# Pooling the keys and values of two batches on TensorE, alpha's load on another queue, and new numbers in the schedule's table

## The chip, the cores and the metric

One core of a Trainium2 chip runs the whole program. The metric is the device time of one execution in microseconds (us), the median of several runs. Engines are named as the profile names them: PE (TensorE), DVE (VectorE), ACT (ScalarE), POOL (GpSimd) and SP, which issues most of the transfers.

## The reference

Attention over pooled keys and values (8 batches, 8 heads, 576 tokens, 64 wide, groups of 8 tokens averaged to 72), then a dense layer pair with a leaky ReLU whose slope alpha is one number per hidden unit, then a layer of 8 experts in which each token goes to one.

```python
k_p = k.reshape(B, H, Sp, pool, D).mean(axis=3)          # 576 -> 72
v_p = v.reshape(B, H, Sp, pool, D).mean(axis=3)
attn = softmax(np.matmul(q, k_p.T) / sqrt(D))
x = np.matmul(attn, v_p)                                  # 4608 x 512
h = x @ w_in                                              # 512 x 2048
x = (max(h, 0) + alpha * min(h, 0)) @ w_out               # 2048 x 512
expert_idx = argmax(x @ w_gate);  gate_w = softmax at expert_idx
out = gate_w * (max(x @ w1[e], 0) @ w2[e])                # 512 x 1024 x 512, e = expert_idx
```

## The kernel before

Every operand of a large product is split into a high and a low float16 part, and each product is three matmuls (high by high, high by low, low by high). The 4608 tokens are 36 tiles of 128; two tiles make a block of 256, of which there are 18. A block's way is: queries scaled and split (tile `qs`), transposed by a DMA (`qT`), scores against the pooled keys (`sc`), eight exponentials on ACT, weights split (`Abuf`), transposed by a DMA (`AT`), the product with the values (`xp`), its split (`xT`), then 16 groups of 12 matmuls into `hp` (line 811), the leaky ReLU on ACT and DVE (`r`, line 829), its split `gT`, and 8 groups of 12 matmuls into `yp` (line 856). The result is split (`x`), transposed (`x2T`), gated (`gp`, `rp`), and its rows are stored to DRAM (`x2d`) with a table of who goes where. After the last block the expert stage gathers 128 rows at a time (`srec`, `x2g`, `x2gT`) and runs lines 1286 and 1304.

Before a block can run, things must be prepared by DVE, POOL and ACT:

- The keys and values of a batch: `plan_batch` loads `raw` (two large halves each for batch 0, eight pieces of one head each for the others), sums 8 rows to one into `kp` (DVE line 439, or POOL lines 443 and 445, whichever the planner picks), takes the largest value over all partitions (`over_all`: DVE `dg`, PE `mp`, line 313), and splits `kp` into `kc` (transposed into `KTb`) and `VSb`, `vlo`.
- `w_in` and `w_out`: `plan_w` rounds the float32 weights in pieces of 128x1024 (`w_in_t`, `w_out_t`: ACT lines 715, 719, 724, DVE lines 727, 731 and 183), finds scales through `over_all`, and splits them (`w_in_hl`, `w_out_hl`).
- The expert weights, spread over the whole first part (`ew`, `eo`, `wsc`).
- alpha and `w_gate`: `alpha_ld`, lines 387 and 389, two loads on SP's queue.

The order of the work on each engine is fixed when the kernel is built. `Plan.emit` is a list scheduler: each piece of work has an engine or a choice of engines, an assumed duration, a key and buffers to acquire and release, and the planner repeatedly takes the piece that can start first by its own clock. Its clock for SP uses the two dictionaries at the top of the file: `ISSUE`, how long SP is held by one issue of a kind, and `LATE`, how much later than the modelled transfer a kind lands. An engine then runs its list strictly in that order, so what the numbers change is the order alone. PSUM holds two buffers with the tag `y`, used by `yp`, and SBUF two with the tag `raw`.

Of the kernel before, what the change touches and what calls it, by code (L numbers as in the profile page):

```python
# [27 lines left out]

ISSUE = {"qT": 1.4, "AT": 1.9, "yT": 1.4, "kT": 1.5, "xT": 1.4, "v": 1.6, "tok": 0.8}
LATE = {"kv": 1.5, "q": 1.0, "ew": 2.5, "st": 1.0, "qT": 1.0, "AT": 1.2, "yT": 1.0, "kT": 0.8, "v": 2.0, "x2": 2.0, "xT": 1.0}  # L30

# [105 lines left out]
def attn_moe_moe_kernel(ctx: ExitStack, tc: tile.TileContext, q, k, v, w_in, w_out, alpha,  # L137
# [217 lines left out]

    o_c1 = add("POOL", 3.6, setup_consts, key=-1000)
    o_c2 = add("POOL", 2.0, setup_consts2, key=0)
# [28 lines left out]
    def alpha_ld():  # L386
        Y.dma_start(out=al1, in_=alpha.rearrange("(m p) -> p m", p=128))
        sm_["g"] = wk.tile([128, KD, NE], F32, tag="wgf", name="g", bufs=1)
        Y.dma_start(out=sm_["g"], in_=w_gate.rearrange("(k p) e -> p k e", p=128))

# [17 lines left out]

    o_al = add("SP", 1.12, alpha_ld, key=-52)
    o_al = add("DVE", tiny(3), alpha_a, [o_al], key=-10)  # L410
# [9 lines left out]
    def plan_batch(b, dl, users):  # L420

        kp, st, raws = [None, None], {}, {}
        red = []
        nc_, pl = (2, "big") if b == 0 else (8, "raw")
        hn = H // nc_
        for w in range(2):
            for c in range(nc_):
# [18 lines left out]
                o = add("SP", dmat(72 * 2048 * hn), load, kind="kv", key=dl - 28 + (8 * w + c) * 8 / nc_, acq=[(pl, 1)])
                red.append(add(EITHER, (0.15 + hn * 0.87, pool(448 * hn) + 0.6), reduce, [o] + red[-1:],
                               key=dl - 26 + (8 * w + c) * 8 / nc_, rel=[(pl, 1)], acq=[("kp", 1)] if c == 0 else []))
# [33 lines left out]
        def vdma():  # L482
            Y.dma_start(out=VS[b][SP_:128, 0], in_=VS[b][0:128 - SP_, 0])
            Y.dma_start(out=VS[b][0:2 * SP_ - 128, 1], in_=VS[b][128 - SP_:SP_, 0])

        osc = {}
        for ws in (((0,), (1,)) if b == 0 else ((0, 1),)):
# [4 lines left out]
            for w in ws:  # L492
                osc[w] = o
        oSK[b], oSV[b] = osc[0], osc[1]
        o = osc[0]
        o1 = add(ANY, his(512), lambda e: s_hi(kc[0:SP_, :, 0, :], kp[0], s_[0], e), [o], key=dl - 7, acq=[("kc", 1)])
        o2 = add(EITHER, stt(512), lambda e: s_lo(kc[0:SP_, :, 1, :], kc[0:SP_, :, 0, :], kp[0], s_[0], e), [o1], key=dl - 6,
                 rel=[("kp", 1)])
        o3 = add("DVE", 0.22, lambda: V.tensor_copy(kc[0:SP_, :, 3, :], kc[0:SP_, :, 0, :]), [o1], key=dl - 6)
        o4 = add("DVE", 0.22, lambda: V.tensor_copy(kc[0:SP_, :, 2, :], kc[0:SP_, :, 1, :]), [o2], key=dl - 5)  # L500
        oKT[b] = add("SP", 1.2, kT, [o2, o3, o4], kind="kT", key=dl - 4 - SPQ, acq=[("KT", 1)], rel=[("kc", 1)])
        o = osc[1]
        o1 = add(ANY, his(512), vhi, [o], key=dl - 4, acq=[("VS", 1)])
        o2 = add(EITHER, stt(512), vlo, [o1], key=dl - 4, acq=[("vlo", 1)], rel=[("kp", 1)])
        o3 = add("SP", 0.5, vdma, [o1], kind="v", key=dl - 4)
        o4 = add("SP", 0.3, lambda: Y.dma_start(out=VS[b][2 * SP_ - 128:3 * SP_ - 128, 1], in_=st["vlo"]), [o2],
                 key=dl - 3, rel=[("vlo", 1)])
# [156 lines left out]
    def plan_w(src, name, col, dl0, dl1, after):  # L664
# [39 lines left out]
        for c in range(8):  # L704
# [72 lines left out]
        for c in range(8):  # L777
# [679 lines left out]
```

## Time and profile before

| | us |
|---|---|
| median of 3 runs (1385.79 to 1389.69) | 1389.04 |
| the profiled execution's own time | 1391.88 |
| its span, first to last instruction | 1390.1 |
| PE busy in the span | 1248.7 (90%) |
| DVE busy | 889.8 (64%) |
| POOL busy | 731.8 (53%) |
| ACT busy | 569.1 (41%) |

The profile is one execution. A busy time counts an engine as busy from an instruction's start to its end; matmuls overlap, so the row of a run of matmuls (its length divided by its count) tells the pace better than the mean of one. "Idle before" is the time in which the engine had nothing running, with the event that ended it. The granted clock is the share of full speed that PE was allowed.

### The profile page before, as it was taken

To read this page: it belongs to the slowest core of one execution; us is meant where nothing else is said; L and a number is where in the kernel's file an instruction comes from. 1 tells how busy PE (TensorE), PEld (TensorE's weight loads), DVE (VectorE), ACT (ScalarE), POOL (GpSimd) and SP (SyncE) were. 2 spreads that over 40 slices of the span, in tenths; PEclk is the share of its full clock that TensorE was granted. 3 is DMA by queue.
4 is the path that set the end of the run, shared out by engine and by line. 5 is a ranking of instruction groups with operands and counts; after the bars stand their busy time and mean duration, and the time that the engine had idled before them with its cause. 6 is when DMAs were issued, how large, how long until landed. Compare 5 with 4: busy or idle time off the path is not lost. (4 is left out here: it accounts for less than half of the span.)

```text
span 1390.1 us, 30446 instructions
## 1 busy us (share of the span) xinstructions
PE 1248.7 (90%) x11555; PEld 868.0 (62%) x11555; DVE 889.8 (64%) x2039; ACT 569.1 (41%) x1309; POOL 731.8 (53%) x788
## 2 busy tenths in 40 slices
PE   0158899999999998999999999998999999999996
PEld 0147465765676565577657766675676776776774
DVE  6999888977888895898878776752432322322321
ACT  3887455545555364566546645530010110110110
POOL 7899757676678577678655655441212212122111
PEclk9999999999999999999999999998999999999999
DMA  9983595896897778778766746539379533883325
GB/s 242 295 239 73 115 243 130 189 234 136 178 221 177 157 183 168 167 183 236 177 143 160 187 125 158 131 91 307 82 206 267 146 77 76 240 260 82 85 66 191
DMA packets 314502, 237.19 MB, mean 171 GB/s; under 512 B 258351, under 2 KB 267695, under 8 KB 309488
## 3 DMA queue, kind: packets, MB, share of 16 engines
q1 hardware_dynamic: 306800, 214.98, 62.6%
q0 software_dynamic: 7552, 20.23, 4.7%
q8 instruction: 92, 1.51, 0.5%
q14 instruction: 58, 0.48, 0.1%
HBM read 263.52 MB, written 54.34 MB: 229 GB/s over the span
## 5 line engine op out<-in xcount | busy, mean ns | idle before, releaser
L811 PE MATMUL hp<-xT,w_in_hl 128*128 128x256 f16 x3456 | 395.9, 275 | 6.2 <-DVE r L829 3.9
L856 PE MATMUL yp<-w_out_hl,gT 128*128 128x512 f16 x1728 | 388.8, 383 | 1.2 <-DVE x L203 1.2
L811 PEld LDWEIGHTS <-w_in_hl 128*128 128x128 f16 x3456 | 336.6, 99 | 53.3 <-issue 6.8
L856 PEld LDWEIGHTS <-gT 128*128 128x128 f16 x1728 | 167.1, 99 | 201.6 <-issue 12.8
L1286 PE MATMUL hp<-x2gT,ws 128*128 128x128 f16 x3744 | 217.6, 221 | 9.8 <-DMA x2gT<-x2g 7.5
L1286 PEld LDWEIGHTS <-ws 128*128 128x128 f16 x3744 | 215.4, 99 | 14.9 <-DMA ws<-wsc 5.6
L1304 PE MATMUL op<-ws,ht 128*128 128x512 f16 x936 | 206.0, 380 | 0.0
L1292 ACT ACTIVATE hr<-hp 128x512 f32<-128x512 f32 x78 | 46.6, 597 | 368.9 <-PE hp L1286 356.8
L842 POOL TENSOR_TENSOR gT<-r,gT 128x512 f16<-128x512 f32 x101 | 121.5, 1207 | 74.1 <-ACT gT L837 70.9
L1304 PEld LDWEIGHTS <-ht 128*128 128x128 f16 x936 | 90.9, 98 | 105.9 <-issue 1.0
L1261 POOL DMA_INDIRECT x2g<-x2d,srec x41 | 44.8, 1092 | 190.7 <-DMA srec<-table 87.5
L829 DVE SCALAR_TENSOR_TENSOR r<-r,al,hp 128x256 f32<-128x256 f32 x288 | 123.2, 470 | 20.7 <-ACT r L825 20.3
L443 POOL TENSOR_TENSOR raw<-raw 72x256 f32<-72x256 f32 (+3 forms) x150 | 115.7, 772 | 38.8 <-DMA raw<-in_v_dram 17.2
L580 ACT ACTIVATE e<-sc,nb,esc 128x72 f32<-128x72 f32 x288 | 116.3, 418 | 46.5 <-DVE nb L572 19.3
L188 ACT ACTIVATE eo<-ew,es 128x512 f16<-128x512 f32 x125 | 83.6, 715 | 117.4 <-DMA wsc<-eo 44.2
L1314 POOL DMA_INDIRECT out_dram<-so,srec x39 | 40.0, 1026 | 165.3 <-DVE so L1311 60.1
L1296 DVE CAST ht<-hr 128x512 f16<-128x512 f32 x78 | 33.6, 431 | 143.3 <-ACT hr L1292 135.0
L1311 DVE TENSOR_SCALAR so<-op,cb 128x512 f32<-128x512 f32 x39 | 29.3, 751 | 144.3 <-PE op L1304 138.4
L837 ACT ACTIVATE gT<-r 128x512 f16<-128x512 f32 x142 | 89.6, 633 | 65.3 <-DVE r L829 31.7
L825 ACT ACTIVATE r<-hp 128x512 f32<-128x512 f32 x144 | 86.1, 599 | 64.7 <-PE hp L811 33.8
L206 POOL TENSOR_TENSOR eo<-ew,eo 128x512 f16<-128x512 f32 x71 | 87.5, 1232 | 5.9
L205 POOL TENSOR_SCALAR ew<-ew,es 128x512 f32<-128x512 f32 x71 | 53.0, 746 | 60.4 <-ACT eo L188 59.9
(227 smaller groups left out, 1477.4 us busy)
## 6 DMA issues: line engine op xcount, KB each, us to landing
ws<-wsc SPq DMA_DIRECT2D x166, 1024.0 KB
ew<-in_moe_w_dram SPq DMA_DIRECT2D x32, 1024.0 KB
wsc<-eo SPq DMA_DIRECT2D x64, 512.0 KB
x2d<-x SPq DMA_DIRECT2D x36, 256.0 KB
qr<-in_q_dram SPq DMA_DIRECT2D x32, 256.0 KB
w_in_f<-in_moe_w_in_dram SPq DMA_DIRECT2D x16, 512.0 KB
w_out_f<-in_moe_w_out_dram SPq DMA_DIRECT2D x16, 512.0 KB
raw<-in_k_dram SPq DMA_DIRECT2D x56, 144.0 KB
```

Source lines behind the costliest of these rows:

```text
L188: A.activation(out=hi, in_=src, func=ACTF.Copy, scale=s)
L206: G.tensor_tensor(out=lo, in0=src, in1=hi, op=ALU.subtract)
L443: G.tensor_tensor(out=r[:, :, 0:n], in0=r[:, :, 0:n], in1=r[:, :, n:2 * n], op=ALU.add)
L580: A.activation(out=c["e"][x], in_=c["scv"][x], func=ACTF.Exp, bias=c["nb"][:, z // 4, z % 4:z % 4 + 1], scale=c["esc"], accum_out=c["sm"][x])
L811: T.matmul(out=hp, lhsT=wt[:, a, kk, (m % 4) * 128:(m % 4 + 1) * 128], rhs=xTt[j][:, x, kk, :], start=(n == 0), stop=(n == 3 * KD - 1))
L825: A.activation(out=c["r"], in_=hps[j, m // 2], func=ACTF.Relu, scale=-1.0)
L829: V.scalar_tensor_tensor(out=c["r"][:, z], in0=c["r"][:, z], scalar=al1[:, m - 1 + z:m + z], in1=hps[j, m // 2][:, z], op0=ALU.mult, op1=A ...
L837: A.activation(out=gT[j][0][:, n2], in_=c["r"], func=ACTF.Copy)
L842: on(eng).tensor_tensor(out=gT[j][1][:, n2], in0=c["r"], in1=gT[j][0][:, n2], op=ALU.subtract)
L856: T.matmul(out=ypt[i], lhsT=gT[j][x][:, m, o_ * 128:(o_ + 1) * 128], rhs=W["w_out"][part][:, w, m % 4, :], start=(m == 0 and x == 0 and w ...
L1286: T.matmul(out=hp[:, f, :], lhsT=ws[kk // 2][:, kk % 2, a, ff * 128:(ff + 1) * 128], rhs=c["xT"][:, x * KD + kk, :], start=(z == 0), stop= ...
L1304: T.matmul(out=op, lhsT=c["ht"][:, x, f, :], rhs=ws[f // 4][:, f % 4, w, :], start=(f == 0 and x == 0 and w == 0), stop=(f == KF2 - 1 and ...
```

## The change

Four things are changed.

1. The pooling of batches 0 and 1 is done by PE: eight matmuls with a 72x72 float32 identity (`idf`) add the eight rows of a group in PSUM (`pool_pe`). The sum lies in a `y` buffer (`kpp`) until it is split. As it is in PSUM, POOL takes no part in the split: the high parts may go to DVE or ACT, the low parts go to DVE.
2. alpha and `w_gate` are loaded from ACT's queue, first thing.
3. The identity `idf` is made by POOL from `idb`, and stays in one of two `x2T` buffers until batch 1 is pooled.
4. The numbers of the planner's table and a few assumed durations are others. They change no instruction, only the order and, where there is a choice, the engine.

```diff
-ISSUE = {"qT": 1.4, "AT": 1.9, "yT": 1.4, "kT": 1.5, "xT": 1.4, "v": 1.6, "tok": 0.8}
-LATE = {"kv": 1.5, "q": 1.0, "ew": 2.5, "st": 1.0, "qT": 1.0, "AT": 1.2, "yT": 1.0, "kT": 0.8, "v": 2.0, "x2": 2.0, "xT": 1.0}
+ISSUE = {"qT": 1.3, "AT": 3.5, "yT": 1.3, "kT": 1.4, "xT": 1.3, "v": 1.6, "v2": 0.85, "tok": 0.4}
+LATE = {"kv": 1.2, "q": 2.0, "ew": 2.1, "st": 1.0, "qT": 0.5, "AT": 2.2, "yT": 0.5, "kT": 0.2, "v": 3.3, "v2": 1.4, "x2": 0.5, "xT": 1.0}
...
+    NPE = 2
+    PEK = 100.0
...
     def stt(n):
-        return dve(n) + 0.02, 0.2 + n * (PHI + PTT)
+        return dve(n) + 0.15, 0.25 + n * (PHI + PTT)
...
+        idf.append(wk.tile([SP_, SP_], F32, tag="x2T", name="idf", bufs=2))
+        G.tensor_copy(idf[0], idb[0:SP_, 0:SP_])
...
     def alpha_ld():
-        Y.dma_start(out=al1, in_=alpha.rearrange("(m p) -> p m", p=128))
+        A.dma_start(out=al1, in_=alpha.rearrange("(m p) -> p m", p=128))
...
-        Y.dma_start(out=sm_["g"], in_=w_gate.rearrange("(k p) e -> p k e", p=128))
+        A.dma_start(out=sm_["g"], in_=w_gate.rearrange("(k p) e -> p k e", p=128))
...
-    o_al = add("SP", 1.12, alpha_ld, key=-52)
+    o_al = add("ACT", 7.0, alpha_ld, key=-1000, lat=2.0)
...
+        by_pe = b < NPE
...
+                def pool_pe(w=w, c=c):
+                    if c == 0:
+                        kp[w] = ps_y.tile([128, DM], F32, tag="y", name="kpp")[0:SP_].rearrange("p (h d) -> p h d", d=D)
+                    r = raws.pop((w, c))
+                    for i in range(PL):
+                        T.matmul(out=kp[w][:, hn * c:hn * c + hn, :], lhsT=idf[0], rhs=r[:, :, i * D:(i + 1) * D],
+                                 start=(i == 0), stop=(i == PL - 1))
...
+                if by_pe:
+                    red.append(add("PE", pe(8, 4 * hn * D * 1.3), pool_pe, [o, o_c1] + red[-1:], key=dl - 26 + (8 * w + c) * 8 / nc_ - PEK,
+                                   rel=[(pl, 1)] + ([("x2T", 1)] if b == NPE - 1 and w == 1 and c == nc_ - 1 else []),
+                                   acq=[("y", 1)] if c == 0 else [], lat=0.15))
+                    continue
-                red.append(add(EITHER, (0.15 + hn * 0.87, pool(448 * hn) + 0.6), reduce, [o] + red[-1:],
+                red.append(add(EITHER, (0.15 + hn * 0.87, pool(448 * hn) + 0.95), reduce, [o] + red[-1:],
...
+        kpr = [("y" if by_pe else "kp", 1)]
+        en, en2 = (ANY, EITHER) if not by_pe else (("DVE", "ACT"), "DVE")
```

**The start of SP's queue.** Here stand K and V of batch 0 (`raw`), the first two query tiles (`qr`), alpha (`al`), `w_gate` (`g`) and the first weights (`w_in_f`). Before:

```order
L431 DMA raw_113<-in_k_dram 72x4x512
L431 DMA raw_115<-in_k_dram 72x4x512
L534 DMA qr<-in_q_dram 128x8x64 x2
L387 DMA al_88<-in_moe_alpha_dram 128x16x1
L389 DMA g<-in_moe_w_gate_dram 128x4x8
L431 DMA raw_135<-in_v_dram 72x4x512
L431 DMA raw_145<-in_v_dram 72x4x512
L692 DMA w_in_f_170<-in_moe_w_in_dram 128x4x256 x2
```

With the change:

```order
L438 DMA raw_118<-in_k_dram 72x4x512
L438 DMA raw_120<-in_k_dram 72x4x512
L561 DMA qr<-in_q_dram 128x8x64 x2
L438 DMA raw_137<-in_v_dram 72x4x512
L438 DMA raw_154<-in_v_dram 72x4x512
L719 DMA w_in_f_158<-in_moe_w_in_dram 128x4x256 x2
L561 DMA qr<-in_q_dram 128x8x64
```

The two small loads are gone from SP, where they stood ahead of V and of `w_in`; they are ACT's first two rows.

**PE's queue from its start to the first groups of the first block.** `kpp` is a pooled sum (x8 is one group of eight matmuls, 72x256 a half of batch 0, 72x64 one head of batch 1), `mp` a largest value over partitions, `xp` attention times values, `hp` the first layer. With the change:

```order
L458 MATMUL kpp<-raw_118,idf 72x256 x8
L458 MATMUL kpp<-raw_120,idf 72x256 x8
L315 LDWEIGHTS ones
L315 MATMUL mp<-dg,ones 128x256
L458 MATMUL kpp<-raw_137,idf 72x256 x8
...
L647 MATMUL xp<-AT,VSb 64x128
L458 MATMUL kpp<-raw,idf 72x64 x16
L838 LDWEIGHTS w_in_hl
L838 MATMUL hp<-xT,w_in_hl 128x256
...
L458 MATMUL kpp<-raw,idf 72x64 x8
L838 LDWEIGHTS w_in_hl
```

Before, PE's queue begins with `mp` and has no row of this kind. Of the sixteen groups of batch 1, seven stand ahead of the first `hp` and nine among the `hp` rows of the first two blocks, each in PE's fixed order behind the load of its piece.

**SP's queue at the change from the last block to the experts.** `srec` is the table's row list for one gather, `x2T` the last block's transpose for the gate, `x2gT` a gathered tile's transpose, `ws` the expert weights. Before:

```order
L1254 DMA srec<-table 128x2
L889 DMA_TRANSPOSE x2T<-x_12635 128x8x128
L1274 DMA_TRANSPOSE x2gT<-x2g 128x8x128 x2
...
L1248 DMA ws_1_12697<-wsc 128x4096
L892 DMA x2d<-x_12635 128x1024
...
L1254 DMA srec<-table 128x2
L889 DMA_TRANSPOSE x2T<-x_12756 128x8x128
```

With the change:

```order
L1281 DMA srec<-table 128x2
L916 DMA_TRANSPOSE x2T<-x_12702 128x8x128
...
L1281 DMA srec<-table 128x2
L919 DMA x2d<-x_12702 128x1024
L1301 DMA_TRANSPOSE x2gT<-x2g 128x8x128 x2
L916 DMA_TRANSPOSE x2T<-x_12842 128x8x128
...
L1275 DMA ws_1_12862<-wsc 128x4096
```

The later `srec` loads, which stood behind weights and the store of `x2d`, now stand ahead of them (five in a row between the two `x2T`), and the last `x2T` stands ahead of the second walk's weights.

## Rows read from the trace of the kernel before

**Rows 1.** Busy by stage: length, PE PEld DVE ACT POOL, clock, DMA share, GB/s.

```profile
0.00:88.70 88.70, 8.58 (x104) 6.86 (x105) 75.66 (x129) 55.73 (x97) 72.64 (x81) 1.00 1.01 265
88.70:160.00 71.30, 62.95 (x504) 47.42 (x504) 68.74 (x115) 48.23 (x77) 62.59 (x56) 0.94 0.40 99
160.00:620.00 460.00, 431.99 (x3574) 287.72 (x3573) 377.15 (x907) 245.62 (x634) 322.22 (x383) 0.98 0.81 185
620.00:940.00 320.00, 316.35 (x2623) 214.99 (x2622) 235.12 (x595) 171.48 (x422) 187.13 (x189) 1.00 0.61 156
940.00:1000.00 60.00, 50.20 (x511) 37.05 (x510) 20.30 (x71) 6.24 (x11) 12.61 (x12) 0.89 0.73 211
1000.00:1390.00 390.00, 378.62 (x4245) 274.01 (x4243) 112.84 (x227) 41.82 (x71) 74.67 (x70) 0.99 0.55 152
```

**Rows 2.** Timeline of PE, 60 to 90: start, length, work, idle before, releaser.

```profile
79.20 1.12 PE L561 MATMUL sc<-KTb,qT 128*128 128x72 f16 x16 [10.46 <-ACT e L580]
...
85.40 1.06 PE L620 MATMUL xp<-AT,VSb 128*64 128x128 f16 x16 [2.59 <-DVE mr L316]
...
88.77 1.44 PE L811 MATMUL hp<-xT,w_in_hl 128*128 128x256 f16 x6 [1.25 <-DVE xT L203]
```

**Rows 3.** DVE by shape, 0 to 90: count, busy us, mean ns, idle before.

```profile
L439 DVE TENSOR_REDUCE kp<-raw 72x256 f32<-72x2048 f32 x2 | 7.2, 3610 | 6.3 <-DMA raw<-in_k_dram 6.3
...
L309 DVE TENSOR_SCALAR dg<-idb,iw 128x128 bf16<-128x128 bf16 x4 | 4.2, 1051 | 0.0
...
L203 DVE SCALAR_TENSOR_TENSOR xT<-xp,xT 128x512 f16<-128x512 f32 x2 | 1.4, 680 | 0.0
...
L439 DVE TENSOR_REDUCE kp<-raw 72x64 f32<-72x512 f32 x1 | 1.0, 1015 | 0.0
```

**Rows 4.** The page's groups: POOL's pooling.

```profile
L443 POOL TENSOR_TENSOR raw<-raw 72x256 f32<-72x256 f32 (+3 forms) x150 | 115.7, 772 | 38.8 <-DMA raw<-in_v_dram 17.2
```

**Rows 5.** Timeline of SP, 0 to 30.

```profile
3.95 4.95 SPq L387 DMA_DIRECT2D al<-in_moe_alpha_dram  x1
8.94 1.71 SPq L389 DMA_DIRECT2D g<-in_moe_w_gate_dram  x1
...
11.68 2.59 SPq L692 DMA_DIRECT2D w_in_f<-in_moe_w_in_dram  x3
```

**Rows 6.** Timeline of DVE, one row, at 30.87.

```profile
30.87 0.24 DVE L309 TENSOR_SCALAR dg<-idb,kvm 128x128 bf16<-128x128 bf16 x1
```

**Rows 7.** Timeline of PE: one shape early and late, and a run of scores.

```profile
15.41 0.37 PE L313 MATMUL mp<-dg,ones 128*128 128x256 bf16 x1 [15.41 <-DVE inv L281]
...
139.70 0.27 PE L313 MATMUL mp<-dg,ones 128*128 128x256 bf16 x1
...
208.05 0.68 PE L561 MATMUL sc<-KTb,qT 128*128 128x72 f16 x16
```

**Rows 8.** The page's groups: weight loads of PE.

```profile
L811 PEld LDWEIGHTS <-w_in_hl 128*128 128x128 f16 x3456 | 336.6, 99 | 53.3 <-issue 6.8
```

**Rows 9.** Timeline of PE, 140 to 172.

```profile
141.12 10.52 PE L856 MATMUL yp<-w_out_hl,gT 128*128 128x512 f16 x48
...
156.01 1.12 PE L561 MATMUL sc<-KTb,qT 128*64 128x72 f16 x16 [3.74 <-DMA KTb<-kc]
157.07 10.37 PE L856 MATMUL yp<-w_out_hl,gT 128*128 128x512 f16 x36
```

**Rows 10.** Waits of PE, 160 to 620: total us, times, longest us.

```profile
PE xp L620 <- DMA AT<-Abuf: 8.5, 5, 4.4
PE mp L313 <- DVE xT L203: 6.1, 4, 3.6
PE rp L973 <- DVE oh L945: 5.5, 4, 1.8
```

**Rows 11.** What POOL waited for, 930 to 1000.

```profile
POOL x2g L1261 <- DMA srec<-table: 35.6, 4, 16.6
```

More of the change, by code (lines that the diff above doesn't have):

```diff
@@ L331, in key_out @@
         return (32 * (i // 2) + 16 if i > 3 else 32 + 16 * (i // 2)) + 8 * (i % 2)
+    idf = []
     def setup_consts():
@@ L354, in setup_consts2 @@
         G.memset(Sacc, 0.0)
-    o_c1 = add("POOL", 3.6, setup_consts, key=-1000)
+    o_c1 = add("POOL", 3.6, setup_consts, key=-1000, acq=[("x2T", 1)])
     o_c2 = add("POOL", 2.0, setup_consts2, key=0)
@@ L484, in vdma, with st_ @@
             Y.dma_start(out=VS[b][0:2 * SP_ - 128, 1], in_=VS[b][128 - SP_:SP_, 0])
+        kpr = [("y" if by_pe else "kp", 1)]
+        en, en2 = (ANY, EITHER) if not by_pe else (("DVE", "ACT"), "DVE")
+        dhi = his(512) if not by_pe else his(512)[1::-1]
+        dlo = stt(512) if not by_pe else stt(512)[0]
+        def st_(f):
+            return f if not by_pe else lambda: f("DVE")
         osc = {}
@@ L495, in plan_batch @@
         o = osc[0]
-        o1 = add(ANY, his(512), lambda e: s_hi(kc[0:SP_, :, 0, :], kp[0], s_[0], e), [o], key=dl - 7, acq=[("kc", 1)])
-        o2 = add(EITHER, stt(512), lambda e: s_lo(kc[0:SP_, :, 1, :], kc[0:SP_, :, 0, :], kp[0], s_[0], e), [o1], key=dl - 6,
-                 rel=[("kp", 1)])
+        o1 = add(en, dhi, lambda e: s_hi(kc[0:SP_, :, 0, :], kp[0], s_[0], e), [o], key=dl - 7, acq=[("kc", 1)])
+        o2 = add(en2, dlo, st_(lambda e: s_lo(kc[0:SP_, :, 1, :], kc[0:SP_, :, 0, :], kp[0], s_[0], e)), [o1], key=dl - 6,
+                 rel=kpr)
         o3 = add("DVE", 0.22, lambda: V.tensor_copy(kc[0:SP_, :, 3, :], kc[0:SP_, :, 0, :]), [o1], key=dl - 6)
@@ L502, in plan_batch @@
         o = osc[1]
-        o1 = add(ANY, his(512), vhi, [o], key=dl - 4, acq=[("VS", 1)])
-        o2 = add(EITHER, stt(512), vlo, [o1], key=dl - 4, acq=[("vlo", 1)], rel=[("kp", 1)])
+        o1 = add(en, dhi, vhi, [o], key=dl - 4, acq=[("VS", 1)])
+        o2 = add(en2, dlo, st_(vlo), [o1], key=dl - 4, acq=[("vlo", 1)], rel=kpr)
         o3 = add("SP", 0.5, vdma, [o1], kind="v", key=dl - 4)
-        o4 = add("SP", 0.3, lambda: Y.dma_start(out=VS[b][2 * SP_ - 128:3 * SP_ - 128, 1], in_=st["vlo"]), [o2],
+        o4 = add("SP", 0.3, lambda: Y.dma_start(out=VS[b][2 * SP_ - 128:3 * SP_ - 128, 1], in_=st["vlo"]), [o2], kind="v2",
                  key=dl - 3, rel=[("vlo", 1)])
@@ L739, in plan_w @@
             if by_dve:
-                o = add("DVE", dve(1024), f2, [o3], key=key - 2, rel=[("eo", 1)])
+                o = add("DVE", dve(1024) + 0.2, f2, [o3], key=key - 2, rel=[("eo", 1)])
                 o = add("DVE", dve(1024), f2b, [o], key=key - 2, rel=[(tk, 1), ("big", 1)])
@@ L794, in plan_w @@
             o = p1 = add(ANY, his(1024), hi, [o_sc, p1], key=first(key - 1, 122), acq=[("big", 1)] if c % 2 == 0 else [])
-            o = add(EITHER, stt(1024), lo, [o], key=first(key - 1, 91), rel=[("big", 1)] if c % 2 == 1 else [])
+            o = add(EITHER, (1.55, 3.95), lo, [o], key=first(key - 1, 91), rel=[("big", 1)] if c % 2 == 1 else [])
             oW[name] += [o, o]
```

## The prediction

> **What bounds the kernel now.** I read the busy time by stage first, then PE's waits and timeline in each stage, because every stage has another limit [rows 1]. Up to 88.7 us PE is busy for 8.6: it has nothing to multiply until the first two tiles of `xT` exist. In that stretch DVE is busy 75.7 of 88.7 and POOL 72.6, and the DMA engines are full (share 1.01). From 88.7 to 160 PE is busy 62.9 of 71.3, DVE 68.7. From 160 to 620 PE is busy 432.0 of 460 and DVE 377.2. From 620 on PE is all but full, save for the change to the experts (50.2 of 60) and the tail. So PE's idle time is 80.1 + 8.3 + 28.0 + 3.7 + 9.8 + 11.4 = 141 us, and what the change is worth is what it takes out of these, less what it adds to PE where PE is full.
>
> The first product starts at 88.77, released by DVE's write of the second `xT` [rows 2]. The `xp` ahead of it stood at 85.40 behind other rows of PE's queue, and the scores at 79.20 behind ACT's exponentials. DVE is nevertheless the engine to count: it hardly rests, and each of those steps waits for a DVE row somewhere.
>
> **Part A, the start.** The change takes from DVE, ahead of the second `xT`, two sums of 3.61 and one of 1.02 [rows 3], and adds the two residuals `kc` and `vlo`, now from PSUM, for which I take the residual of `xT` from PSUM, 0.68 each [rows 3]: -8.2 + 1.4 = -6.9. Other rows change sides too, by the table of numbers; pricing those that differ by their shape's mean, they give back about 1.9 (two multiplications of `e` and a high part of `w_in` leave; the first rows of `w_out` come forward). Net on DVE: -5. DVE starts later: its first rows used to be ready when K landed at 6.3 [rows 3]; now it begins with the table's rows, which wait for POOL's constants, at about 8 by my estimate: +2. Against that, SP loses 4.95 + 1.71 = 6.7 us of issue ahead of V and `w_in` [rows 5], so that `w_in`, issued at 11.68 before, goes out some 6 us earlier. ACT, where the two loads now stand, had no work in that time, so there they cost nothing; if an exponential or a `qs` stood behind them, they would cost up to those 6.7. The transfers are limited by the engines that carry them, so I count 3 of the 6.7. Sum: -5 + 2 - 3 = **-6** (bounds 0, if the exponentials on ACT set the pace, and -12, if all of SP's 6.7 and DVE's 5 come through).
>
> The four large groups on PE cost nothing as long as PE waits there anyway. They could make K late: at the start PE takes 0.37 for a 128x256 float16 product that takes 0.27 at 139.70 [rows 7], 0.10 more, as 256 columns take at 1.2 and not 2.4 GHz (256/1.2 - 256/2.4 = 107 ns), though the clock column has 1.00 there [rows 1]. DVE needs 3.61 for one half of K [rows 3]; eight matmuls of four times 256 columns at the slow level would be 6.8 us for a half, 4 x 256 / 1.2 each. The second half can't start before POOL's or DVE's did, so K could come some us later; but K's next steps stood behind V's sums on DVE, which are gone, so I count nothing.
>
> On how DVE and POOL hinder each other the rows say this: a `dg` takes 1.05 on the mean of the first 90 us and 0.24 alone [rows 3, 6]. POOL loses all of batch 0 and 1, sixteen pieces of two adds of 0.77 and one more add [rows 4], so DVE may also be held less. I leave it out of the sum; it is a rival below. The Trainium skill (SBUF — State Buffer, who interferes with whom) says that the port pair which DVE and GpSimd share is an exclusive lock, held for a whole instruction, so that the later one blocks fully. By that rule DVE's rows would shrink as POOL's go, and the start would come earlier than my sum has it; the two `dg` rows agree with it.
>
> **Part B, 88.7 to 160.** Nine groups of batch 1 now stand in PE's queue among the first products. No row of the trace is a float32 matmul. The nearest is a run of scores, sixteen matmuls of 72 columns in 0.68, 0.042 each with the weight loads hidden [rows 7]. Lower bound: as that, 8 x 0.042 = 0.34 a group. Upper bound: four times the columns (the factor that the new planner line has) and every weight load of 0.099 [rows 8] in the open, 8 x 4 x (0.042 + 0.099) = 4.5. I take 1.2, near four times the score row (1.36), because in the score row the loads are hidden: 9 x 1.2 = +11. Against it: PE's 8.3 us of waits in this stretch are partly filled by just these groups, and batch 1's keys are ready earlier. Its `KTb` now costs a wait of 3.74, after which 36 products took 10.37, 0.288 each, while 48 ran at 0.219 each just before [rows 9]: 2.5 us more, with the granted clock of the stretch at 0.94 [rows 1]. So 10.8 us are to be had there; I take -9. Sum of B: **+2** (bounds -6 and +32). The added wait is for the load of each piece; behind it in PE's queue stands everything. And the two `y` buffers are held by the sums until DVE's `kc` and `vlo` are written, so the first `yp` waits for those: 132 `hp` matmuls stand between the last group and that `yp`, so I count nothing.
>
> **Part C, 160 to 620.** PE's waits there are 28.0 us [rows 1], above all for `AT` (8.5), for `mp` behind `xT` (6.1) and for `rp` behind the gate's DVE rows (5.5) [rows 10]. The new numbers give a transpose of `AT` 3.5 of SP's time and 2.2 of lateness, so the planner puts more products between the scores and `xp`. Counting PE's matmuls in both orders, that distance grows by about 1 us for most tiles, and the one between `gp` and `rp` by about as much. Waits of 1.5 on the mean are cut, not removed: I take a fifth, **-6** (bounds -14, half of them, and +5, since every list is reordered and new waits may come).
>
> **Part D, the change to the experts.** PE idles 9.8 us there [rows 1]; POOL's gathers wait 35.6 us for `srec`, once 16.6 [rows 11]. The `srec` loads now go out ahead of weights and stores. A gather that is earlier helps PE only if its transpose is too: **-3** (bounds -8 and +4).
>
> Sum: -6 + 2 - 6 - 3 = **-13**, and 1391.9 - 13 = 1379 for the profiled execution. That execution was 2.8 above the median of the runs shown, so against the median: 1389 - 13 = **1376**.
>
> **Rivals.**
> - *The start is paid back.* PE is the limit from 88.7 on, so the 11 us of float32 work come off the gains of A, and the new order brings C and D nothing: -6 + 11 - 5 = 0, **1389**. For it: PE is busy 88% in B; the DMA engines are full, so the earlier `w_in` may land no earlier. Against it: DVE, which holds the waits of B, loses work.
> - *Slower: the weight loads of the float32 matmuls lie open.* A group then costs 4.5 and nine 40: -6 + 40 - 9 - 6 - 3 = +16, **1405**. It decides from about 2.7 us a group, where nine groups eat the 24 us that the other terms give. For it: a group alternates eight small products with eight loads of the same identity, and loads have no cheaper row than 0.099 [rows 8]. Against it: the score row hides a load per 0.042 [rows 7]. The Trainium skill (TensorE: Matmul & The Clock Gate, weight-path perf modes) has a rule against this change: fast weight load is off when the type is float32. By it, loads would be dearer than those of the score row; no row here shows one.
> - *POOL's relief sets DVE free.* If DVE's rows shrink as in [rows 6] against [rows 3], four `dg` alone give 3.2 before the start, and the pieces that are longer beside POOL as much again: A becomes -12, B -4, C -8, D -3: -27, **1362**. For it: batch 1's adds on POOL alone are up to 16 x 2 x 0.77 = 25 us [rows 4]. Against it: POOL takes up other rows at once, since the planner gives it what is free.
>
> **How the numbers follow.** A measurement of this kernel tells about 0.3% (4.2 us) from no change. The forecast has 0.50, the third rival 0.20, the first 0.16, the second 0.14. So faster 0.71, same 0.15, slower 0.14. The range reaches from the third rival with 2 us more, 1360, to the first rival and the upper bounds of C or D, 1396; it leaves out the full second rival, and some of the forecast's tails.
>
> **What would show it.** Right: the first `hp` released at 80 to 85 by the second `xT`; groups of `kpp` of about 1.2 us at 72x64, with waits for their loads under 1 us; the wait for `KTb` at 156 gone; PE's idle time from 160 to 620 at 20 to 24; POOL's waits for `srec` under half. Wrong: a first `hp` at 88 or later; groups over 2.7 us; PE waiting for `raw`, or `yp` for `vlo`; or more idle time on PE after 160 than 28.

## The result, and the profile after

The change is slower: its runs lie at 1.0085 of the runs of before, 95% interval 1.0061 to 1.0109, with a median of 1402.29 us (1400.41 to 1404.54, four runs) against 1387.41. The forecast was 1376, its range ended at 1396. The profiled execution took 1400.41 us with a span of 1398.5, 8.4 more than the span of before. The medians lie further apart, since the profiled execution of before (1391.88) lies above its listed runs; the account that follows sets spans against spans.

The change by stage (columns as in [rows 1]; the first stage ends where the first run of `hp` starts, at 95.79 instead of 88.77):

```profile
0.00:95.70 95.70, 49.34 (x279) 35.30 (x280) 70.43 (x138) 62.24 (x112) 57.75 (x63) 1.00 1.00 261
95.70:160.00 64.30, 63.07 (x633) 53.12 (x632) 58.02 (x101) 42.92 (x61) 48.28 (x35) 1.00 0.37 91
160.00:620.00 460.00, 433.10 (x3565) 289.74 (x3564) 371.72 (x897) 249.33 (x640) 300.70 (x356) 0.99 0.81 182
620.00:940.00 320.00, 310.53 (x2606) 212.66 (x2605) 238.38 (x586) 170.03 (x419) 187.99 (x195) 0.99 0.63 156
940.00:1000.00 60.00, 47.55 (x436) 32.81 (x434) 23.21 (x88) 5.87 (x12) 13.55 (x14) 0.89 0.74 211
1000.00:1390.00 390.00, 389.97 (x4368) 281.89 (x4366) 115.93 (x233) 43.55 (x73) 75.07 (x71) 1.00 0.55 148
```

And `kpp` alone, the pooling on PE, over the first 160 us:

```profile
0.00:50.00 50.00, 27.88 (x64) 15.23 (x64) 2.77 (x4) 1.34 (x2) 1.00 1.02 243
50.00:95.70 45.70, 14.27 (x112) 13.73 (x112) 0.00 (x0) 0.00 (x0) 1.00 0.97 280
95.70:160.00 64.30, 11.05 (x147) 10.59 (x145) 2.85 (x4) 1.25 (x2) 1.00 0.37 91
```

So the pooling takes 53.2 us of PE. PE's idle time up to 160 was 88.5 [rows 1] and is 46.4 + 1.2 = 47.6: 40.9 of the 53.2 lie in it. Behind 160 PE idled 52.9 and idles 57.4 (26.9 + 9.5 + 12.5 + 0.0, and 8.5 in the tail). PE's other work is 8.3 shorter (1240.4 against 1248.7). 53.2 - 40.9 + 4.5 - 8.3 = +8.5, the 8.4 of the spans. (The mean granted clock of the profiled executions was 0.987 with the change and 0.983 before, so the clock isn't what the change lost.)

Most of the idle time that is new lies between 590 and 740; before, and with the change:

```profile
590.00:740.00 150.00, 147.06 (x1275) 102.73 (x1274) 124.88 (x305) 87.25 (x225) 104.36 (x114) 1.00 0.73 182
...
590.00:740.00 150.00, 137.54 (x1128) 92.61 (x1127) 126.01 (x293) 76.74 (x195) 99.99 (x122) 0.98 0.76 170
```

PE idles 12.5 us there instead of 2.9.

PE's timeline of the change at the start:

```profile
6.70 13.90 PE L458 MATMUL kpp<-raw,idf 72*72 72x256 f32 x32 [6.70 <-DMA raw<-in_k_dram]
...
20.61 7.03 PE L458 MATMUL kpp<-raw,idf 72*72 72x256 f32 x16
...
27.54 7.05 PE L458 MATMUL kpp<-raw,idf 72*72 72x256 f32 x16
...
79.23 0.26 PE L315 MATMUL mp<-dg,ones 128*128 128x128 bf16 x1 [6.48 <-DVE xT L203]
79.86 4.10 PE L458 MATMUL kpp<-raw,idf 72*72 72x64 f32 x32 [0.37 <-DMA raw<-in_k_dram]
83.75 1.17 PE L588 MATMUL sc<-KTb,qT 128*128 128x72 f16 x16
89.30 1.07 PE L647 MATMUL xp<-AT,VSb 128*64 128x128 f16 x16 [4.37 <-DMA AT<-Abuf]
91.89 4.11 PE L458 MATMUL kpp<-raw,idf 72*72 72x64 f32 x32 [1.53 <-DMA raw<-in_k_dram]
95.79 6.62 PE L838 MATMUL hp<-xT,w_in_hl 128*128 128x256 f16 x48
102.25 1.20 PE L458 MATMUL kpp<-raw,idf 72*72 72x64 f32 x16
```

Each float32 matmul shows as two records, so x16 is one group of eight. Scores that stood at 79.20, `xp` at 85.40 and `hp` at 88.77 [rows 2] now stand at 83.75, 89.30 and 95.79, with two groups of batch 1 (4.1 us) ahead of the scores and two more, behind a wait for `raw`, ahead of `hp`.

What PE waited for from 160 to 620 (columns as in [rows 10]):

```profile
PE gp L947 <- DMA x2T<-x: 13.8, 6, 4.3
PE xp L647 <- DMA AT<-Abuf: 3.6, 3, 1.8
PE hp L838 <- DVE r L856: 3.0, 3, 1.8
PE rp L1000 <- DVE oh L972: 2.6, 3, 1.1
```

The same from 620 to 1000:

```profile
PE hp L1313 <- DMA x2gT<-x2g: 8.5, 1, 8.5
PE gp L947 <- DMA x2T<-x: 7.7, 2, 4.4
```

The waits of [rows 10] are down (`AT` 8.5 to 3.6, `rp` 5.5 to 2.6, `mp` behind `xT` gone), and one has grown that was small before: `gp`, the gate, waits for its `x2T`. From 160 to 620 before, and in the stretch from 590 to 740 of the change, where it makes up most of the 12.5 us:

```profile
PE gp L920 <- DMA x2T<-x: 3.7, 2, 2.1
...
PE gp L947 <- DMA x2T<-x: 9.2, 3, 4.4
```

### The profile page after: what moved, and what is told of

The parts are those of the page before. It is cut to its first block, busy times and chain, and to the rows that moved or that the text cites. A ratio compares the mean times of both kernels' runs of the same rounds, so it can differ in the third digit from the quotient of the medians.

```text
span 1398.5 us, 31059 instructions
## 1 busy us (share of the span) xinstructions
PE 1293.6 (92%) x11875; PEld 905.5 (65%) x11875; DVE 878.4 (63%) x2039; ACT 573.9 (41%) x1313; POOL 684.3 (49%) x731
## 4 chain that ended last, share of the span: by engine, by line
PE 61%; DMA 14%; DVE 13%; POOL 4%; issue 4%; SPq 2%; ACT 2%; POOLq 0%; ACTq 0%; DVEq 0%
PE hp L1313 14%; PE hp L838 14%; PE op L1331 14%; PE yp L883 13%; DMA x2T<-x 4%; PE kpp L458 3%; DMA ew<-in_moe_w_dram 2%; DVE r L856 2%; DMA qr<-in_q_dram 2%; DMA AT<-Abuf 1%; DVE em L183 1%; DMA table<-rec,pu 1%; DMA wsc<-eo 1%; DVE kp L446 1%; DMA raw<-in_k_dram 1%
## 5 line engine op out<-in xcount | busy, mean ns | idle before, releaser
L883 PE MATMUL yp<-w_out_hl,gT 128*128 128x512 f16 x1728 | 383.6, 379 | 0.4 <-DVE x L203 0.4
L1313 PE MATMUL hp<-x2gT,ws 128*128 128x128 f16 x3744 | 217.0, 221 | 12.5 <-DMA x2gT<-x2g 8.5
L450 POOL TENSOR_TENSOR raw<-raw 72x256 f32<-72x256 f32 (+1 forms) x128 | 87.2, 682 | 42.6 <-DMA raw<-in_v_dram 20.3
L183 DVE TENSOR_REDUCE em<-ew 128x1 f32<-128x1024 f32 x64 | 76.9, 1205 | 11.3 <-DMA ew<-in_moe_w_dram 11.1
L203 DVE SCALAR_TENSOR_TENSOR eo<-ew,es,eo 128x512 f16<-128x512 f32 x69 | 65.6, 959 | 22.5 <-ACT eo L188 18.3
```

Source lines behind the costliest of these rows:

```text
L183: V.tensor_reduce(out=o, in_=i, axis=axis, op=ALU.max, apply_absolute_value=True)
L883: T.matmul(out=ypt[i], lhsT=gT[j][x][:, m, o_ * 128:(o_ + 1) * 128], rhs=W["w_out"][part][:, w, m % 4, :], start=(m == 0 and x == 0 and w ...
L1313: T.matmul(out=hp[:, f, :], lhsT=ws[kk // 2][:, kk % 2, a, ff * 128:(ff + 1) * 128], rhs=c["xT"][:, x * KD + kk, :], start=(z == 0), stop= ...
```

## The experiments

Each kernel was timed against the kernel before on the same chip; ratios are to before, with 95% intervals.

### The parts alone

The new numbers (`ISSUE`, `LATE` and the durations of five operations), the pooling, and alpha's move, each put into the kernel before by itself:

```diff
-ISSUE = {"qT": 1.4, "AT": 1.9, ...}
+ISSUE = {"qT": 1.3, "AT": 3.5, ...}
```

> The kernel before with the new numbers of the schedule alone (issue and lateness tables and the durations of five operations); pooling stays on VectorE and GpSimd, alpha on SyncE. Theory N (the numbers cost the time): 1397 to 1405 us, TensorE waits for `x2T` ahead of `gp` 15 us or more (before 3.7, after 21.5), the transition around 960 us slower too. Theory P (the pooling on TensorE costs the time, the numbers are a help or nothing): 1378 to 1388 us, waits for `x2T` under 8 us, first `hp` near 88.8 us as before.

Measured: 1.0029 (1.0012 to 1.0047), a median of 1392.51 us, waits for `x2T` 12.5 us (here and below, summed from 160 to 950). Between the two theories.

```diff
+    NPE = 2
...
+                if by_pe:
+                    red.append(add("PE", pe(8, 4 * hn * D * 1.3), pool_pe, ...
```

> The kernel before with the pooling of two batches on TensorE alone; old numbers, alpha on SyncE. Theory P: 1397 us or more, first `hp` 7 us later than before (95 to 97 us), waits for `raw` ahead of `kpp` some 20 us as in the change. Theory N: 1383 to 1390 us; first `hp` is late by 7 us too, but that is caught up by 550 us and nothing is lost behind 600 us (`x2T` waits under 6 us).

Measured: 1.0088 (1.0062 to 1.0114). First run of `hp` at 90.83, not 95 to 97; waits for `raw` 11.4, for `x2T` 12.8. Theory P has the time, but not by its reasons.

```diff
-        Y.dma_start(out=al1, in_=alpha.rearrange("(m p) -> p m", p=128))
+        A.dma_start(out=al1, in_=alpha.rearrange("(m p) -> p m", p=128))
...
-    o_al = add("SP", 1.12, alpha_ld, key=-52)
+    o_al = add("ACT", 7.0, alpha_ld, key=-1000, lat=2.0)
```

> The kernel before with the loads of alpha and w_gate on ScalarE's queue alone. Both theories and the trace of the change (the second load of values then took 5.8 us to issue, the first load of w_in came 0.2 us earlier): 1385 to 1390 us, first `hp` at 87 to 90 us. My forecast had 3 us from this part: first `hp` at 85.8 us would be that.

Measured: 1.0033 (1.0013 to 1.0053), `hp` at 88.57: no 3 us at the start, and a loss that neither theory had.

```diff
-    NPE = 2
+    NPE = 1
```

> The change with only batch 0 pooled on TensorE (batch 1 on VectorE and GpSimd again); the new numbers and alpha's move stay. Theory W (batch 1's sixteen groups, waiting for `raw` in TensorE's order, are what delays the start): first `hp` at 86 to 90 us, waits ahead of `kpp` under 3 us, time 1392 to 1397 us. Theory C (batch 0's sums at the slow clock delay it): first `hp` at 92 to 96 us still. Theory N adds that the time behind 600 us is lost all the same, so 1395 us or more either way.

Measured: 1.0217 (1.0186 to 1.0248), `hp` at 97.65. Half of the pooling taken back made it much slower. W falls. C's late start is there, and later than it said; N's bound of 1395 us is passed; neither says why this kernel should be 18 us slower than the change. The parts cost 0.29, 0.88 and 0.33% alone and 0.85 together: they don't add.

### A price, and a control

```diff
-ISSUE = {... "yT": 1.3 ...}   LATE = {... "yT": 0.5, "x2": 0.5 ...}
+ISSUE = {... "yT": 1.4 ...}   LATE = {... "yT": 1.0, "x2": 2.0 ...}
```

> The change with three numbers of the new table put back (issue of the `x2T` transposes 1.4, their lateness 1.0, lateness of the `x2` stores 2.0). Theory G (these numbers put `gp` into TensorE's order before its `x2T` has landed, and the waits cost time): waits of `gp` for `x2T` fall from 21.5 to under 6 us, and the time to 1388 to 1396 us. Rival theory R (each new order is a new draw; the wait is only where the lateness of this order happens to show): the `x2T` waits fall, but others take their place and the time stays within 3 us of the change's, 1399 to 1405 us.

Measured: 1.0119 (1.0081 to 1.0157). The waits for `x2T` fell from 21.5 to 12.5, those of `hp` for `r` grew from 3.4 to 10.8. G falls. R's forecast holds at the median (1403.24), but these six runs spread from 1391 to 1410.

```diff
-                    for i in range(PL):
+                    for i in range(PL if b == 0 else 2 * PL):
...
-                                 start=(i == 0), stop=(i == PL - 1))
+                                 start=(i % PL == 0), stop=(i % PL == PL - 1))
```

> The change, with the eight matmuls of each of batch 1's sixteen groups done twice (the second eight start the sum anew, so the result is the same; the order is unchanged). Theory A (from the first `hp` on TensorE is the bound, so what it is given there is paid in full): nine groups at 1.03 to 1.2 us behind the first `hp` are 9 to 11 us, and of the seven ahead of it, at 2.1 us, half or more is paid: 1412 to 1425 us in all. Rival H (the groups lie in idle time that the loads of `raw` set): 1402 to 1406 us, with the waits for `raw` shorter by what the groups are longer.

Measured: 1.0190 (1.0171 to 1.0210), a median of 1413.11; against the change 1.0190 / 1.0085, +14.6 us. `kpp` of this kernel, ahead of its first run of `hp` (now at 101.73 instead of 95.79) and behind it:

```profile
0.00:101.73 101.73, 55.63 (x288) 42.34 (x288) 2.77 (x4) 1.35 (x2) 1.00 0.93 247
101.73:160.00 58.27, 20.32 (x290) 19.85 (x289) 1.80 (x3) 1.25 (x2) 1.00 0.35 85
```

Ahead of `hp` the groups take 13.5 us more than in the change (55.63 - 42.15), and 5.9 of it delay `hp`; behind it they take 9.3 more (20.32 - 11.05). Together that is 15.2, about the 14.6 of the runs. (The profiled execution, the longest of its runs, was 21.6 us longer; in it the waits for `x2T` are 5.9 longer too, 27.4 instead of 21.5.) Theory A holds and H falls: what PE is given from the first `hp` on is paid in full, as long as the order is held.

```diff
-                red.append(add(EITHER, (0.15 + hn * 0.87, pool(448 * hn) + 0.6), reduce, ...
+                red.append(add(EITHER, (0.15 + hn * 0.87, pool(448 * hn) + 0.95), reduce, ...
```

> A control: the kernel before with one number of its schedule changed that describes nothing new (a sum on GpSimd 0.35 us dearer). Theory R (any new order costs some us, since the old one was the best of many): 1390 to 1396 us, with waits in other places than before. If new orders as such cost nothing: 1385.5 to 1389 us.

Measured: 1.0109 (1.0090 to 1.0128). One number of the schedule, with no operation added, moved or removed by hand, costs 15 us, as much as the change or more (the intervals overlap).

```diff
 (the pooling alone, as above)
-    NPE = 2
+    NPE = 1
```

> The kernel before with batch 0 alone pooled on TensorE; old numbers, alpha on SyncE, batch 1 on VectorE and GpSimd. Theory C (batch 0's sums on TensorE take 14 us for keys that VectorE and GpSimd did in 8, so the start is later): first `hp` at 92 to 96 us, time 1391 to 1398 us. Theory A alone (only the work behind the first `hp` costs): first `hp` at 87 to 90 us, time 1383 to 1389 us. Theory G has the 1415 us of the kernel with one batch and new numbers come from the numbers: this one is then over 15 us faster than that.

Measured: 1.0069 (1.0050 to 1.0088), `hp` at 91.71. Nearer to C than to A alone, and 20 us faster than its fellow with the new numbers (1.0217).

### Four more pairs that differ by the pooling alone

If one number shifts the time by 15 us, a single pair can't price the pooling. So the pooling was put beside the control's number, alpha's move and the new numbers, and taken out of the change:

```diff
 (the pooling alone, and beside it in turn)
+    ... pool(448 * hn) + 0.95), reduce ...
+    o_al = add("ACT", 7.0, alpha_ld, key=-1000, lat=2.0)
+ISSUE = {"qT": 1.3, "AT": 3.5, ...}
 (the change)
-    NPE = 2
+    NPE = 0
```

> Pooling on TensorE, and of the numbers only the control's one (a sum on GpSimd 0.35 us dearer). Its partner without pooling on TensorE is the control, 1.0109 of before. Three theories on the four pairs of this call, each pair alike but for the pooling: (D) the pooling costs 12 us in every order, so all four pooled kernels are 0.8 to 0.9% slower than their partners; (A) it costs about what its groups take behind the first `hp` less what it saves, 0.2 to 0.6% as a mean over the pairs; (R) it costs nothing, and the mean is 0 within 0.2%. Here: D 1.019, A 1.010 to 1.016, R 1.003 to 1.016.

> Pooling on TensorE with alpha on ScalarE's queue, old numbers. Partner: the kernel with alpha's move alone, 1.0033. D 1.012, A 1.005 to 1.010, R 1.0 to 1.007 with the four pairs' mean at no difference.

> Pooling on TensorE with the new numbers, alpha on SyncE. Partner: the kernel with the numbers alone, 1.0029. D 1.012, A 1.005 to 1.009, R 1.0 to 1.007 with the four pairs' mean at no difference.

> The change without its pooling on TensorE (new numbers and alpha's move alone). Partner: the change, 1.0085. D 1.000, A 1.002 to 1.006, R 1.003 to 1.013.

| beside it | sums on VectorE and GpSimd | two batches on PE | ratio of the two |
|---|---|---|---|
| nothing | 1 (before) | 1.0088 | 1.0088 |
| the control's number | 1.0109 | 1.0044 (1.0019 to 1.0070) | 0.9936 |
| alpha's move | 1.0033 | 1.0097 (1.0064 to 1.0129) | 1.0064 |
| the new numbers | 1.0029 | **0.9953 (0.9928 to 0.9978)** | 0.9924 |
| numbers and alpha | 1.0046 (1.0020 to 1.0072) | 1.0085 (the change) | 1.0039 |

The mean of the lower four pairs is 0.9991, of all five 1.0010. D falls: two of the four pooled kernels are faster than their partners. The mean is where R has it, but the pairs spread by 0.75% (one standard deviation of the five), so five of them leave the mean open by 0.9% to either side, and A's 0.2 to 0.6% isn't excluded. What they show is that no price of the pooling stands out from what a new order does.

This doesn't contradict the doubled groups: from 95 to 160 PE idles 7.5 to 10.8 us in the five kernels on the left and 0.3 to 2.8 on the right: most of the 11 us that the nine groups take lies in time in which PE waited before.

The first run of `hp` is later in all but one: 88.8, 90.8, 88.6, 88.9 and 85.6 on the left, 90.8, 90.8, 93.6, 93.0 and 95.8 on the right, 4.3 us on the mean. One kernel is faster than both: the change without alpha's move, median 1380.41 (1373.79 to 1388.23, twelve runs), 0.5% under before and 1.3% under the change. Its stages:

```profile
0.00:95.70 95.70, 54.47 (x308) 39.23 (x309) 69.64 (x140) 60.20 (x112) 55.23 (x62) 1.00 0.99 253
95.70:160.00 64.30, 64.02 (x635) 52.70 (x634) 59.30 (x109) 48.99 (x78) 46.76 (x42) 1.00 0.48 111
160.00:620.00 460.00, 439.43 (x3626) 292.17 (x3625) 383.26 (x923) 248.82 (x628) 322.06 (x395) 0.99 0.83 187
620.00:940.00 320.00, 316.43 (x2609) 214.92 (x2607) 227.33 (x588) 165.94 (x412) 177.36 (x173) 1.00 0.60 162
```

PE idles 41.2, 0.3, 20.6 and 3.6 us in these, where the change idles 46.4, 1.2, 26.9 and 9.5. Over the whole spans (1375.5 and 1398.5) idle time makes up 20.0 of the 23.0 us between them, PE's busy time 3.0; the granted clock, 0.989 and 0.987, hardly differs.

### The queue, or the order that comes with it

Between the fast kernel and the change lie 18 us and alpha's two loads. These two kernels exchange the queue alone; every other instruction of every engine stands as it stood:

```diff
 (the faster kernel)
-        Y.dma_start(out=al1, in_=alpha.rearrange("(m p) -> p m", p=128))
+        A.dma_start(out=al1, in_=alpha.rearrange("(m p) -> p m", p=128))
```

> The faster kernel (pooling on TensorE, new numbers, alpha on SyncE: 0.9953 of before) with the two loads of alpha and w_gate issued on ScalarE's queue, and the order of every engine else left as it was. Theory Q (the queue costs the time: the loads of values follow sooner and meet others): 1.005 or more. Theory O (the order costs it, the queue nothing): 0.994 to 0.998, 1377 to 1383 us.

Measured: 0.9963 (0.9937 to 0.9988).

```diff
 (the change: the two loads leave alpha_ld)
+                    sh = [SP_, hn, PL * D]; (b, w, c) == (0, 1, 0) and alpha_sp()
```

> The change with alpha and w_gate issued on SyncE's queue, at the place that they have there in the kernel before (behind the second `qr`, ahead of the values), and the order of every engine else left as the change has it. Theory Q: 0.993 to 0.999, the gain of the kernel with alpha on SyncE comes back. Theory O: 1.006 to 1.011, as the change.

Measured: 1.0071 (1.0045 to 1.0097). Theory O, twice: the queue is worth 0.1% either way, inside the intervals, and the order about 1.2%.

```diff
 (the faster kernel)
-... pool(448 * hn) + 0.95), reduce ...
+... pool(448 * hn) + 0.6), reduce ...
```

> A second control: the faster kernel with one number put back (a sum on GpSimd 0.35 us cheaper in the plan, as it was before). Theory R (each order is a draw, with a spread of some 0.5%): anywhere from 0.997 to 1.012, and above 0.998 more likely than not. Rival W (the pooling with the new numbers is worth 5 us whatever the order): 0.993 to 0.998.

Measured: 1.0047 (1.0032 to 1.0062): R again. The fast kernel's gain is lost with one number of the plan, the same one as in the first control.

```diff
 (the faster kernel)
-        by_pe = b < NPE
+        by_pe = b == 1
```

> The faster kernel with batch 1 alone pooled on TensorE; batch 0 on VectorE and GpSimd as before. Theory C (batch 0's sums at the slow clock, done at 20.6 us in place of 15, delay the start): first `hp` at 86 to 90 us, 4 us or more earlier than in the faster kernel (93.0). Rival: batch 1's groups in TensorE's order do, and first `hp` stays at 92 us or later. Its time is a draw of an order again: 0.99 to 1.01.

Measured: 0.9958 (0.9936 to 0.9980), with the first run of `hp` (at 87.12) where C has it:

```profile
81.31 1.07 PE L647 MATMUL xp<-AT,VSb 128*64 128x128 f16 x16
84.93 0.37 PE L838 MATMUL hp<-xT,w_in_hl 128*128 128x256 f16 x1 [2.55 <-ACT xT L188]
87.12 2.51 PE L838 MATMUL hp<-xT,w_in_hl 128*128 128x256 f16 x11 [1.82 <-DVE xT L203]
89.42 1.78 PE L458 MATMUL kpp<-raw,idf 72*72 72x64 f32 x16
```

### Is the new wait the loss?

In both orders `gp` was held back by some 5 us of PE's work, with what hangs on it; the orders of ACT, POOL and SP stay as they were.

```diff
...
+            if o.kind == "gp" and not held:
+                room = 5.0 + o.dur
+            if o.kind == "gp" or any(u is o for h, _ in held for u, _ in h.users):
+                held.append((o, (name,) if both else ()))
...
```

> The change with each `gp` (and what hangs on it on VectorE) emitted some 5 us of TensorE's work later; the order of ScalarE, GpSimd and SyncE is the same, VectorE's differs by a place or two around the gate. Theory G (the waits of `gp` for `x2T` hold up ready `hp` behind them, and that is what this order loses): the waits fall from 21.5 to under 5 us and the time by 10 to 15 us, 0.998 to 1.002. Rival S (the waits are a sign: VectorE and the transposes are late, and TensorE runs out of work soon after): the waits fall as well, others grow by as much, 1.006 to 1.010.

> The faster kernel (0.9953) with each `gp` emitted 5 us later in the same way. Theory G: the waits for `x2T` fall from 8.3 to under 3 us, the time by 4 to 6 us, 0.990 to 0.993. Rival S: 0.994 to 0.998.

Measured: 1.0160 (1.0129 to 1.0190) and 1.0018 (0.9997 to 1.0039), both about 0.7% slower than without. PE's waits of the first from 160 to 950:

```profile
PE rp L1010 <- DVE oh L982: 21.2, 11, 4.5
PE hp L848 <- DVE r L866: 8.2, 7, 2.2
```

The waits for `x2T` are gone (0.3 us), and `rp`, which needs what DVE makes of `gp`, waits 21.2 instead of 3.3 (in the second kernel 13.8 instead of 2.0). G falls; S holds in that the wait moves, though it too had expected no loss. The gate stands between two deadlines, and this order has no room there. Nor do the waits for `x2T` rank the orders: the control has 6.3 us of them at 1.0109, its fellow with the pooling 16.3 at 1.0044, and the change without its pooling 13.9 at 1.0046. What makes one order better than another stays open: their idle time differs in many waits of 1 to 4 us.

## Why the prediction was wrong

The stages below are marked by the first `hp` and by the first `gp` of blocks 1, 9 and 16, which start 7.0 later, 3.0 later, 2.4 earlier and 9.8 later than before (212.9, 599.5 and 929.2 against 209.9, 601.9 and 919.4); such marks carry some us of their own, as the order around them changes.

| step | forecast | measured in the profiled pair |
|---|---|---|
| A, to the first `hp` | -6 | +7.0 |
| B, to block 1 | +2 | -4.0 |
| C, to block 9 | -6 | -5.4 |
| (no term) to block 16 | 0 | +12.2 |
| D, to the end | -3 | -1.4 |
| sum | -13 | +8.4 |

The middle marks depend on the block: at block 8 the change is 2.5 us earlier than before, at block 10 it is 6.1 later. Counted by the `hp` and `yp` products done, the change is 4.5 us ahead where before stood at 591 and 9.4 behind where it stood at 729: the loss behind block 9 lies where the new idle time lies.

**A is the first step that failed** (-6 forecast, +7.0 measured). Only its +2 for DVE's later start came (first row at 8.37 instead of 6.29). DVE did lose its sums, but it could not use the time that this left in the first 50 us. DVE by shape in the first 50 us of before (columns as in [rows 3]):

```profile
L727 DVE SCALAR_TENSOR_TENSOR w_in_t<-wc,w_in_t 128x1024 int32<-128x1024 int32 x5 | 6.6, 1312 | 0.2 <-ACT w_in_t L719 0.2
L183 DVE TENSOR_REDUCE m<-w_in_t 128x1 f32<-128x1024 f32 x5 | 6.0, 1207 | 0.0
```

The same of the change:

```profile
L754 DVE SCALAR_TENSOR_TENSOR w_in_t<-wc,w_in_t 128x1024 int32<-128x1024 int32 x5 | 6.1, 1215 | 0.0
L183 DVE TENSOR_REDUCE m<-w_in_t 128x1 f32<-128x1024 f32 x4 | 4.8, 1206 | 0.0
...
L183 DVE TENSOR_REDUCE kvm<-kpp 72x1 f32<-72x512 f32 x2 | 1.4, 687 | 8.9 <-PE kpp L458 8.9
```

DVE fell from 37.2 us of work to 25.8 in these 50 us, and did the same five pieces of `w_in` and one maximum less; it now waits 8.9 for PE's sums, which stand in place of its own. I had read that DVE "hardly rests" over the whole stage. Split in two, the stage of before reads otherwise (columns as in [rows 1]):

```profile
0.00:50.00 50.00, 2.13 (x20) 1.48 (x21) 37.16 (x75) 23.80 (x34) 35.73 (x55) 1.00 1.03 250
50.00:95.70 45.70, 13.38 (x126) 10.58 (x126) 45.42 (x65) 38.09 (x82) 43.59 (x35) 1.00 0.97 280
```

The stage of the change:

```profile
0.00:50.00 50.00, 29.53 (x84) 16.79 (x84) 25.83 (x72) 22.74 (x30) 16.99 (x40) 1.00 1.02 243
50.00:95.70 45.70, 19.80 (x195) 18.51 (x196) 44.60 (x67) 39.50 (x83) 40.77 (x23) 1.00 0.97 280
```

Before, DVE is 74% busy in the first 50 us and 99% in the rest: the relief went into the first part, and the second, where DVE was full, is as full in the change (44.6 of 45.7 us). The 3 us that I counted of SP's 6.7 did not come either. SP's timeline of the change:

```profile
1.70 2.72 SPq L561 DMA_DIRECT2D qr<-in_q_dram  x2
4.46 5.80 SPq L438 DMA_DIRECT2D raw<-in_v_dram  x2
11.52 0.94 SPq L719 DMA_DIRECT2D w_in_f<-in_moe_w_in_dram  x2
```

The loads of V took the place and the time of alpha's, and the first `w_in` went out at 11.52 instead of 11.68.

That the four large groups cost nothing is not what the kernels show. Set side by side with equal numbers and an equal queue, batch 0 on PE starts `hp` later each time: 91.7 against 88.8 (old numbers), 93.0 against 87.1 (new numbers, batch 1 on PE in both), 97.7 against 85.6 (new numbers and alpha's move). Batch 1 on PE starts it no later: 90.8 against 91.7, 95.8 against 97.7, 87.1 against 88.9. A new order alone moves this start by up to 5 us (85.6 to 90.8 with nothing pooled on PE), so the sizes are rough, but the signs agree. By which steps the delay passes from K and V (maxima at 20.6 and 34.6, against 15.5 and 28.7) to `hp` isn't shown; the first scores stand at 40.8 against 40.1. The estimate of 6.8 us for a half was right (7.0), and with it the sentence that K could be late, which I then counted as nothing. So A's mechanism failed in two places: a relief was credited where DVE was not the limit, and the time of the four large groups was put at nothing. (The product of 0.37 us behind that estimate is bfloat16 in [rows 7], not float16; the sum doesn't depend on it.)

**B's price was right**: 1.20 a group, and the 3.74 for `KTb` is gone; PE idles 1.2 us instead of 8.3, and waits for no `raw` there (the five waits for `raw`, 19.4 us, all lie ahead of the first `hp`). The nine groups are work that PE must do while it is the limit, as the doubled groups show. The slower rival named 1405, close to the result, by a wrong mechanism: the weight loads of `kpp` are dear (behind the first `hp` 145 ns at the median for 72x72), but they run beside the matmuls (10.6 of the 11.1 us in the last row of `kpp` above), so a group takes 1.20 and not 4.5. Whether loads or columns set the 1.20 isn't shown: eight loads of 145 are 1.16. The Trainium skill (TensorE: Matmul & The Clock Gate, weight-path perf modes) says that fast weight load is off for float32; the trace agrees in that these loads are dearer than the 99 ns of [rows 8], but that decided nothing.

**C's size was right by luck.** Its waits went as forecast, and the `x2T` waits, which no term had, gave most of it back: PE idles 26.9 there, not 20 to 24. The -5.4 of the table rests on the choice of block 9.

**The term that was missing is the largest.** I wrote that "every list is reordered and new waits may come" and gave that 11 us upward in one stage, C, and nothing behind 620, where PE seemed full. The control shows what a new order can cost by itself: 15 us. What the runs put in its place is +12.2 between blocks 9 and 16, most of it idle time, with the waits of `gp` for `x2T` at its head; why this order falls there stays open, since taking those waits out moved the time to `rp`. Five orders with the sums on VectorE and GpSimd span 1 to 1.0109, five with the pooling 0.9953 to 1.0097, and the kernel before is the best of the first five. A forecast whose parts sum to -13 had to be centred on where a new order of this planner lies (1.0054 on the mean of the four others without the pooling on PE, 7 to 8 us, known only now), with some 10 us to either side.

**D:** POOL's long waits for `srec` are gone between 930 and 1000, as forecast, and others stand in their place. PE idles 12.5 us from 940 to 1000, more than the 9.8 of before, so the -1.4 of the table doesn't bear the forecast out. What POOL waits for now:

```profile
POOL x2g L1288 <- DMA x2T<-x: 14.7, 1, 14.7
POOL x2g L1288 <- DMA x2gT<-x2g: 12.9, 3, 12.3
```

**The third rival** (POOL's relief) is half there. In the first 50 us, where POOL's work fell from 35.7 to 17.0 us, DVE's rows shrank: `dg` of `kvm` from 1044 to 242 ns and the pieces of `w_in_t` from 1312 to 1215. By the rule of the Trainium skill (SBUF — State Buffer, who interferes with whom), a port pair held by one engine for a whole instruction, rows that need the pair should shrink where POOL does less; the trace agrees there. Over the whole stage, POOL being nearly as busy behind 50 us as before (40.8 and 43.6), `dg` of `iw` fell from 1051 to 460 ns, while the pieces of `w_in_t` grew from 1384 to 1599. No gain reached `hp`.

## What to carry to other kernels

Where a planner orders the work, the trace prices one order: before pricing a change, perturb a number that should not matter, and take the spread of the times as the least width of any forecast (here 1%, more than each part of this change). A part is then priced by pairs over several orders (five were too few here), or with the order held fixed, as alpha's queue was (0.1%, where the plain comparison of the two kernels said 1.3%). And relief for an engine counts only in the stretch in which that engine is the limit: split the stage where its busy share changes, before crediting it.

## What the runs showed of the hardware

- PE worked without a pause from 6.7 to 34.6 us on float32 sums, and the last of the four took as long as the first pair's halves (7.05 us for eight matmuls of 256 columns). That is 3.4 ns a column, near what four times the columns (the planner's factor) take at the level of 1.2 GHz (3.33), while the row of the stage shows a granted clock of 1.00. A group of 64 columns took 2.05 to 2.18 us up to 95 us, and 1.20 at 102.25, right behind 48 `hp`; the loads of its weights took 240 ns at the median in the first case and 145 in the second.
- alpha's small load, SP's fifth load at the start, took 4.95 us to issue [rows 5]; as ACT's first it took 0.44 us, and SP's fifth was then the first half of V, with 5.25 (the row of 5.80 above is both halves). In all twenty traces SP's fifth load took 4.86 to 5.40 us, whichever load it was: the time belonged to the place in SP's queue, not to the load. `w_gate`, by contrast, took 1.71 us as SP's sixth and 3.85 as ACT's second:

```profile
0.81 0.44 ACTq L393 DMA_DIRECT2D al<-in_moe_alpha_dram  x1
1.28 3.85 ACTq L395 DMA_DIRECT2D g<-in_moe_w_gate_dram  x1
```
